# Decoding the weights of nine FFN blocks during the attention, with a stop in DRAM

## The chip, the cores and the metric

The kernel runs on one core of one Trainium2 chip. The metric is device time in microseconds (us) of one execution; before the change its median is 1493.73 us over 3 runs (1490.55 to 1495.77). A profile is one more execution, recorded by the hardware profiler.

## The reference

Three layers follow each other: causal attention in blocks of 64 (8 batches, 8 heads, 576 tokens, 64 wide), a gated convolution, and a Fourier mixing layer with an FFN.

```python
scores = where(block_i >= block_j, q @ k.T / sqrt(64), -1e9)
attn = exp(scores - max) / (sum + 1e-9)
x = attn @ v                                  # 8 x 576 x 512
gate = sigmoid(causal 5-tap convolution of x with conv_w)
x = (gate * (x @ w_val)) @ w_out
u = x + real(fft2(x))                         # over tokens and channels
un = (u - mean(u)) / sqrt(var(u) + 1e-6)
out = u + relu(un @ w_ch1) @ w_ch2            # 512 -> 2048 -> 512
```

The weights arrive as float64, so the program reads each as a pair of 32-bit words. The FFN's weights are w_ch1 (512 x 2048) and w_ch2 (2048 x 512); the hidden width of 2048 is cut into 16 blocks of 128.

## The kernel before, in words

The program has two phases. **Phase 1** is attention, gated convolution and Fourier mixing. Two heads form a pair; 32 pairs of 9 units each give 288 units (`NU`), and the loop over n at L936 walks them. One pass of the loop emits for unit n the scores (`emit_qk`, TensorE), and for units some passes behind the maximum (`emit_max`, VectorE), the exponential (`emit_exp`, ScalarE) and the transposes (`emit_t`, TensorE, copied out by ScalarE). In the ninth unit of a pair `emit_av` multiplies with the values. Before it, `emit_recip` makes the reciprocals on VectorE, and `emit_factors` transposes them on TensorE, copies them to a tile rt, and sends them through DRAM to XF. When the 4 pairs of a batch (36 units) are done, `dense(b)` is queued: the value and output products, the transforms and the store of u to DRAM (`u_d`). Its pieces are taken into the loop by `step`, so one batch's attention runs beside the previous batch's dense part. `tick` lets chains of small stages (`Chain`) go one stage further; it is called twice per unit, and so a unit has two halves. The queries of a pair are split into high and low parts in one buffer, QHL, and copied from there by DMA: to QQ by `spread` in units 4 and 8 of the pair before, to QD (two buffers, used by the ninth unit) by the last stage of `split` (L351). Kernel-wide, SyncE issues nearly all DMAs, one after the other, and each one waits in that queue for what it needs.

**Phase 2** is the FFN over 9 groups of 512 tokens. `load_u` loads u, `norm` normalises it, and the loop at L1133 goes over 16 blocks f: twelve matmuls into psh (L1143 to L1145, three for each quarter of the channels, because high and low parts are multiplied separately), relu into hh (ScalarE, L1148) and the rest hl (VectorE, L1149), and twelve matmuls into the output (L1161 to L1163) one block later. The weights stay in SBUF for all groups. They are prepared in the first group by `load_w(f)`, called two blocks ahead: a DMA brings 128 x 1024 words (rw, three buffers), `decode` turns them into 128 x 512 float32 (st, three buffers), a ScalarE copy makes the high part and a VectorE subtraction (L1055) the low one. Each block has two such tiles, W1 and W2.

`decode` puts the float32 bits together from the two words of a float64: VectorE shifts the high word (L72), adds bits of the low word (L74) and the sign and exponent bit (L76), and clears values that are too small (L84), by a magnitude that ScalarE makes of the high word (L80). That is four VectorE operations and one on ScalarE for a tile of 128 x 512.

The order of instructions on each engine is made at compile time by a planner that works by priorities (program order) and planned times. So phase 2's first loads and decodes stand between the last operations of phase 1, where memory is free for them. On the chip each engine then takes its instructions strictly in that order.

Of the kernel before, what the change touches and what calls it, by code (L numbers as in the profile page):

```python
# [8 lines left out]
F32 = mybir.dt.float32  # L9
# [8 lines left out]
def kernel(  # L18
# [46 lines left out]
    def decode(raw, dst, mag):  # L65
# [5 lines left out]
        def bits():  # L71
            nc.vector.tensor_scalar(out=d, in0=hi, scalar1=3, scalar2=0x3FFFFFFF,  # L72
                                    op0=ALU.logical_shift_left, op1=ALU.bitwise_and)
            nc.vector.scalar_tensor_tensor(out=d, in0=lo, scalar=29, in1=d,  # L74
                                           op0=ALU.logical_shift_right, op1=ALU.bitwise_or)
            nc.vector.scalar_tensor_tensor(out=d, in0=hi, scalar=-0x40000000, in1=d,  # L76
                                           op0=ALU.bitwise_and, op1=ALU.bitwise_or)

        def size():
            nc.scalar.activation(out=mag, in_=hf, func=AF.Abs)  # L80

        def guard():

            nc.vector.scalar_tensor_tensor(out=dst, in0=mag, scalar=2.0 ** -15, in1=dst,  # L84
                                           op0=ALU.is_ge, op1=ALU.mult)
        def whole():
            bits()
            guard()
        return [size, whole]
# [4 lines left out]
    f_d = [dram.tile([10, P], F32, name=f"f_d{i}") for i in range(2)]  # L94

# [6 lines left out]
    def phase1():  # L102
        with ExitStack() as c1:
# [15 lines left out]
            QD = [pa.tile([P, 2, P], F32R, name=f"QD{i}") for i in range(2)]  # L119
# [9 lines left out]
            cw = pa.tile([P, 4, 5], F32, name="cw")  # L129

# [204 lines left out]
            def split(p):  # L335
# [15 lines left out]
                def q_last():  # L351
                    for r in rs:
                        nc.sync.dma_start(out=QD[p % 2][r, :, r].bitcast(F32), in_=QHL[r, :, D:S].bitcast(F32))

# [37 lines left out]
            def emit_qk(n):  # L392
# [21 lines left out]
                for k0, w in ((0, 320), (320, 256)):  # L414
                    t = sc_tile(n)
                    mm3(t[:, 0:w], QD[p % 2][:, 0], QD[p % 2][:, 1], KP[p][:, k0:k0 + w], KL[p][:, k0:k0 + w], True, True)
# [38 lines left out]
            def emit_recip(p):  # L455

                su = sums[p]
                re = sm.tile([P, 10], F32, tag="re", name="re")
# [9 lines left out]
            def emit_factors(p):  # L468
# [7 lines left out]
                rt = sm.tile([P, P], F32, tag="rt", name="rt", bufs=2)  # L476
# [794 lines left out]
```

## Time and profile before

| | us |
|---|---|
| median of 3 runs | 1493.73 |
| lowest, highest | 1490.55, 1495.77 |
| profiled execution | 1492.41 |
| its span on the core | 1490.6 |
| TensorE busy | 1423.2 (95%) |
| VectorE busy | 829.4 (56%) |
| ScalarE busy | 645.6 (43%) |
| GpSimd busy | 310.0 (21%) |

Times inside the profile count from the start of the span. TensorE's matmuls are pipelined, so one matmul's duration is longer than the time after which the next one starts, and a busy TensorE is not one at its peak; the number of matmuls of one shape in a stretch tells more. The names of tiles are those of the program; L452 is line 452. Phase 1 ends and phase 2 begins between about 600 and 690 us; the two overlap there.

### The profile page before, as it was taken

What the parts mean: (1) busy time and instruction counts of PE and PEld (TensorE: products, weight loads), DVE (VectorE), ACT (ScalarE), POOL (GpSimd) and SP (SyncE); (2) the same over time, 40 slices, a digit from 0 to 9 for tenths busy, and PEclk for the clock granted to TensorE, in tenths of its full rate; (3) what the DMA queues carried; (4) which work ended last, traced back from release to release, by engine and by line L of the source; (5) the groups of instructions that cost most, each with busy time, mean ns of one, the idle gap of its engine ahead of it and who ended that gap; (6) DMA issues with size and microseconds to landing.
All of it is one profiled execution on the core that took longest, in us unless ns stands there. A gap on an engine that the chain in (4) does not pass through costs nothing.

```text
span 1490.6 us, 22931 instructions
## 1 busy us (share of the span) xinstructions
PE 1423.2 (95%) x8543; PEld 1205.1 (81%) x8543; DVE 829.4 (56%) x1668; ACT 645.6 (43%) x1647; POOL 310.0 (21%) x254
## 2 busy tenths in 40 slices
PE   5798999999999999987989999999999999999998
PEld 4567888989898989976768888888888888888887
DVE  6877797979797979599993322232223222222212
ACT  5678777777777777543441212121121212112110
POOL 3423132323232323221001111120111111111100
PEclk9899999999999999999999999999999999999999
DMA  7567665656565655225421010100101000010000
GB/s 216 155 165 191 158 175 151 168 152 168 153 168 152 164 156 137 87 89 173 156 84 57 0 57 0 56 2 1 57 0 57 1 29 29 0 57 0 29 0 29
DMA packets 121290, 137.22 MB, mean 92 GB/s; under 512 B 23502, under 2 KB 91356, under 8 KB 121180
## 3 DMA queue, kind: packets, MB, share of 16 engines
q1 hardware_dynamic: 120640, 135.63, 32.2%
q8 instruction: 67, 1.10, 0.3%
q14 instruction: 43, 0.35, 0.1%
q10 hardware_dynamic: 540, 0.14, 0.0%
HBM read 70.57 MB, written 19.01 MB: 60 GB/s over the span
## 4 chain that ended last, share of the span: by engine, by line
PE 69%; DVE 15%; DMA 5%; ACT 3%; POOL 3%; issue 3%; SPq 2%; DVEq 0%; ACTq 0%; POOLq 0%
PE o L1163 8%; PE o L1161 8%; PE o L1162 8%; PE psh L1144 8%; PE psh L1145 8%; PE psh L1143 8%; PE av L594 4%; PE pt L566 3%; DVE gate L621 2%; PE sc L406 2%; POOL XA L827 1%; PE sc L407 1%; PE psx L165 1%; DVE st L74 1%; DVE mx L438 1%
## 5 line engine op out<-in xcount | busy, mean ns | idle before, releaser
L1149 DVE SCALAR_TENSOR_TENSOR hl<-psh,hh 128x512 fp32r<-128x512 f32 x144 | 99.4, 690 | 392.9 <-ACT hh L1148 392.8
L1148 ACT ACTIVATE hh<-psh 128x512 fp32r<-128x512 f32 x144 | 85.9, 597 | 504.8 <-PE psh L1145 502.8
L1163 PE MATMUL o<-hl,W2H 128*128 128x512 f32 x576 | 221.0, 394 | 14.2 <-DVE hl L1149 14.0
L1145 PE MATMUL psh<-UTH,W1L 128*128 128x512 f32 x576 | 225.4, 391 | 0.9 <-DVE W1L L1055 0.9
L1143 PE MATMUL psh<-UTH,W1H 128*128 128x512 f32 x576 | 224.8, 391 | 0.8 <-ACT UTH L1108 0.8
L1144 PE MATMUL psh<-UTL,W1H 128*128 128x512 f32 x576 | 225.0, 391 | 0.4 <-DVE UTL L1109 0.4
L1161 PE MATMUL o<-hh,W2H 128*128 128x512 f32 x576 | 224.2, 389 | 0.0
L1162 PE MATMUL o<-hh,W2L 128*128 128x512 f32 x576 | 224.0, 389 | 0.0
L452 ACT ACTIVATE PB<-sc,mx 128x128 f32<-128x128 f32 (+4 forms) x320 | 166.7, 526 | 47.2 <-DVE mx L438 27.3
L566 PE MATMUL pt<-ident,PB 128*128 128x128 f32 x800 | 139.7, 282 | 10.9 <-ACT PTb L572 5.2
L1163 PEld LDWEIGHTS o<-hl,W2H 128*128 128x128 f32 x576 | 107.6, 189 | 42.4 <-DVE hl L1149 20.7
L1145 PEld LDWEIGHTS psh<-UTH,W1L 128*128 128x128 f32 x576 | 108.6, 189 | 24.1 <-DVE W1L L1055 1.3
L1143 PEld LDWEIGHTS psh<-UTH,W1H 128*128 128x128 f32 x576 | 108.6, 189 | 24.0 <-ACT UTH L1108 1.1
L1144 PEld LDWEIGHTS psh<-UTL,W1H 128*128 128x128 f32 x576 | 108.6, 189 | 23.6 <-DVE UTL L1109 0.9
L1161 PEld LDWEIGHTS o<-hh,W2H 128*128 128x128 f32 x576 | 108.1, 188 | 22.9 <-ACT hh L1148 0.5
L1162 PEld LDWEIGHTS o<-hh,W2L 128*128 128x128 f32 x576 | 108.2, 188 | 22.6
L621 DVE SCALAR_TENSOR_TENSOR gate<-XF,cw,gate 128x575 f32<-128x575 f32 (+3 forms) x128 | 121.1, 946 | 5.0 <-ACT gate L63 4.2
L566 PEld LDWEIGHTS pt<-ident,PB 128*128 128x128 f32 x800 | 100.8, 144 | 26.9 <-ACT PTb L572 12.0
L1172 POOL TENSOR_TENSOR U<-o,U 128x512 f32<-128x512 f32 x32 | 40.3, 1289 | 365.4 <-DVE o L1170 365.4
L438 DVE TENSOR_REDUCE mx<-sc 128x1 f32<-128x384 f32 (+2 forms) x192 | 104.6, 562 | 4.1 <-PE sc L167 2.1
L406 PE MATMUL sc<-K,QQ 128*128 128x256 f32 (+2 forms) x256 | 87.4, 351 | 16.3 <-DMA QQ<-QHL 13.2
L617 POOL TENSOR_TENSOR XL<-XF,XH 128x576 fp32r<-128x576 f32 x32 | 46.0, 1439 | 256.8 <-ACT XH L57 256.8
(208 smaller groups left out, 2885.8 us busy)
## 6 DMA issues: line engine op xcount, KB each, us to landing
K<-KP SPq DMA_DIRECT2D x128, 144.0 KB, 2.5
QQ<-QHL SPq DMA_DIRECT2D x128, 128.0 KB, 2.5
rw<-in_w_ch SPq DMA_DIRECT2D x32, 512.0 KB, 4.3
VV<-in_v SPq DMA_DIRECT2D x32, 320.0 KB, 3.9
qraw<-in_q SPq DMA_DIRECT2D x32, 288.0 KB, 3.3
kraw<-in_k SPq DMA_DIRECT2D x32, 288.0 KB, 3.4
out<-U SPq DMA_DIRECT2D x36, 256.0 KB, 2.0
QQ<-QHL SPq DMA_DIRECT2D x128, 64.0 KB, 2.8
```

Source lines behind the costliest of these rows:

```text
L406: nc.tensor.matmul(t[:, o:o + w], q[:, 0, m], KK[p][h][:, 0:w], start=True, stop=False)
L438: nc.vector.reduce_max(out=mx[:, j:j + 1], in_=t, axis=AX.X, negate=one)
L452: nc.scalar.activation(out=PB[i][:, k0:k0 + w], in_=t, func=AF.Exp, bias=nm, accum_out=su[:, at + j:at + j + 1])
L566: nc.tensor.transpose(ps[:, j, :], PB[i][:, (j0 + j) * P:(j0 + j + 1) * P], ident)
L621: nc.vector.scalar_tensor_tensor(out=gate[c][:, s:S], in0=XF[:, 0:S - s], scalar=cw[:, c, 4 - s:5 - s], in1=gate[c][:, s:S], op0=ALU.mult, ...
L1143: nc.tensor.matmul(ps, W1H[f][:, c, :], UTH[g][:, c, :], start=(c == 0), stop=False)
L1144: nc.tensor.matmul(ps, W1H[f][:, c, :], UTL[g][:, c, :], start=False, stop=False)
L1145: nc.tensor.matmul(ps, W1L[f][:, c, :], UTH[g][:, c, :], start=False, stop=(c == 3))
L1149: nc.vector.scalar_tensor_tensor(out=l, in0=ps, scalar=0.0, in1=h.bitcast(F32), op0=ALU.max, op1=ALU.subtract)
L1161: nc.tensor.matmul(po[t], W2H[e][:, c], h, start=(e == 0), stop=False)
L1162: nc.tensor.matmul(po[t], W2L[e][:, c], h, start=False, stop=False)
L1163: nc.tensor.matmul(po[t], W2H[e][:, c], l, start=False, stop=(e == NF - 1))
```

## The change

The two tiles of each of the blocks 0 to 8 (`KD = 9`) are decoded in phase 1, as two halves each, which makes 36 half tiles of 128 x 256. A generator, `decode_ahead`, is called twice per unit from unit 62 on (`NW`). For one half tile it issues the DMA of the words into raw_w, passes four calls, then issues the five operations of `decode` one per call, passes one more, issues a DMA of the result to a float32 tile in DRAM (`w_d`), and passes two more. There is one raw_w and one st_w. The magnitude is written over the low words. In phase 2 `load_w` loads st from `w_d` for these blocks and only splits it into high and low part; blocks 9 to 15 are decoded as before. Besides, QD has one buffer, filled in `spread` at unit 8 ahead of the QQ copies; the reciprocals' copy rt lies in XF; and the small tiles su and re have two buffers each where they had six.

```diff
-    def decode(raw, dst, mag):
+    def decode(raw, dst, mag=None):
...
+        m = lo.bitcast(F32) if mag is None else mag
+
         def size():
-            nc.scalar.activation(out=mag, in_=hf, func=AF.Abs)
+            nc.scalar.activation(out=m, in_=hf, func=AF.Abs)
...
-        return [size, whole]
+        return [shifted, low, size, high, guard] if mag is None else [size, whole]
...
+    KD = 9
+    w_d = [[dram.tile([P, D], F32, name=f"w_d{f}{z}") for z in range(2)] for f in range(KD)]
...
-            QD = [pa.tile([P, 2, P], F32R, name=f"QD{i}") for i in range(2)]
+            QD = pa.tile([P, 2, P], F32R, name="QD")
...
+            raw_w = pa.tile([P, D], I32, name="raw_w")
+            st_w = pa.tile([P, D // 2], F32, name="st_w")
...
-                return Chain(k_hi, both(k_dup, k_lo), wait, q_hi, q_lo, q_last)
+                return Chain(k_hi, both(k_dup, k_lo), wait, q_hi, q_lo)
             def spread(p, g):
...
+                if g:
+                    for r in rs:
+                        nc.sync.dma_start(out=QD[r, :, r].bitcast(F32), in_=QHL[r, :, D:S].bitcast(F32))
...
-                    sums[p] = sm.tile([P, 12], F32, tag="su", name="su")
+                    sums[p] = sm.tile([P, 12], F32, tag="su", name="su", bufs=2)
...
-                rt = sm.tile([P, P], F32, tag="rt", name="rt", bufs=2)
                 to, fd = XFS[p % NXF], f_d[p % 2]
+
+                rt = to[:, 0:P]
...
+            def decode_ahead():
+
+                for f in range(KD):
+                    for z in range(2):
+                        for c in range(2):
+                            src = ffn_words(f, z)
+                            if z:
+                                nc.sync.dma_start(out=raw_w, in_=src[:, D * c:D * c + D])
+                            else:
+                                nc.sync.dma_start(out=raw_w.rearrange("p (c f) -> p c f", c=2),
+                                                  in_=src[:, 2 * c:2 * c + 2, :])
+                            for _ in range(4):
+                                yield
+                            for stage in decode(raw_w, st_w):
+                                stage()
+                                yield
+                            yield
+                            nc.sync.dma_start(out=w_d[f][z][:, 256 * c:256 * c + 256], in_=st_w)
+                            yield
+                            yield
...
+            NW = 62
...
+                if n >= NW:
+                    next(ahead_w, None)
...
+                if n >= NW:
+                    next(ahead_w, None)
...
+            for _ in ahead_w:
+                pass
...
                     st = s3.tile([P, D], F32, tag="st", name="st")
...
+                    if f < KD:
+                        nc.sync.dma_start(out=st, in_=w_d[f][z])
+                    else:
+                        rw = rp.tile([P, 2 * D], I32, tag="r", name="rw")
+                        nc.sync.dma_start(out=rw if z else rw.rearrange("p (c f) -> p c f", c=4), in_=ffn_words(f, z))
+                        for stage in decode(rw, st, s4.tile([P, D], F32, tag="mg", name="mg")):
+                            stage()
                     nc.scalar.copy(out=h, in_=st)
```

## Rows read from the trace of the kernel before

**Rows 1.** The profile page: its first line.

```profile
span 1490.6 us, 22931 instructions
```

**Rows 2.** Table of stretches. Columns: stretch, length, each engine busy (instructions), TensorE's clock, DMA.

```profile
350.00:375.00 25.00, 24.55 (x209) 22.86 (x208) 23.51 (x58) 19.56 (x59) 6.37 (x5) 1.00 0.58 148
375.00:400.00 25.00, 25.00 (x229) 22.77 (x229) 15.82 (x39) 20.21 (x63) 4.99 (x5) 1.00 0.62 164
400.00:425.00 25.00, 24.33 (x214) 21.92 (x211) 21.46 (x50) 16.47 (x45) 11.29 (x8) 1.00 0.63 172
625.00:650.00 25.00, 22.59 (x164) 21.32 (x162) 24.00 (x49) 4.55 (x8) 5.90 (x4) 1.00 0.25 88
650.00:675.00 25.00, 23.61 (x155) 20.11 (x153) 24.73 (x46) 13.58 (x32) 7.21 (x5) 1.00 0.24 75
675.00:700.00 25.00, 19.01 (x67) 13.98 (x66) 24.27 (x34) 10.26 (x17) 5.63 (x4) 0.86 0.58 191
700.00:725.00 25.00, 23.08 (x99) 18.05 (x99) 25.00 (x46) 11.60 (x20) 0.00 (x0) 1.00 0.51 172
725.00:750.00 25.00, 22.02 (x95) 17.16 (x94) 24.36 (x45) 10.80 (x19) 0.00 (x0) 1.00 0.45 145
750.00:775.00 25.00, 20.92 (x89) 15.99 (x88) 25.00 (x45) 12.86 (x22) 0.00 (x0) 1.00 0.32 104
800.00:825.00 25.00, 25.00 (x112) 20.69 (x111) 7.46 (x12) 6.03 (x11) 1.33 (x2) 1.00 0.00 1
```

**Rows 3.** The chain of waits, 665 to 775 us: shares by line.

```profile
by line: DVE st L74 14.8%; DVE st L76 14.2%; DVE st L84 10.5%; DVE st L72 8.5%; DVE W1L L1055 7.7%; DVE W2L L1055 6.8%; DVE hl L1149 6.1%; issue 6.0%; DMA rw<-in_w_ch 3.9%; DVE UTL L1109 3.2%; DVE r L1119 3.0%; POOL XA L827 2.7%; DVE q L111
```

**Rows 4.** VectorE in order of time, one FFN block: start, length, line, operation.

```profile
698.76 0.68 DVE L1149 SCALAR_TENSOR_TENSOR hl<-psh,hh 128x512 fp32r<-128x512 f32 x1
...
700.61 0.76 DVE L72 TENSOR_SCALAR st<-rw 128x512 int32<-128x512 int32 x2
701.28 1.28 DVE L74 SCALAR_TENSOR_TENSOR st<-rw,st 128x512 int32<-128x512 int32 x2
702.48 1.29 DVE L76 SCALAR_TENSOR_TENSOR st<-rw,st 128x512 int32<-128x512 int32 x2
703.69 1.29 DVE L84 SCALAR_TENSOR_TENSOR st<-mg,st 128x512 f32<-128x512 f32 x2
704.89 0.69 DVE L1149 SCALAR_TENSOR_TENSOR hl<-psh,hh 128x512 fp32r<-128x512 f32 x1
```

**Rows 5.** Groups of instructions, 675 to 775 us: count, busy, mean ns, idle before.

```profile
L84 DVE SCALAR_TENSOR_TENSOR st<-mg,st 128x512 f32<-128x512 f32 x28 | 19.3, 712 | 0.0
L1163 PE MATMUL o<-hl,W2H 128*128 128x512 f32 x56 | 18.7, 437 | 14.1 <-DVE hl L1149 14.0
L80 ACT ACTIVATE mg<-rw 128x512 f32<-128x512 f32 x26 | 17.4, 671 | 6.3 <-DMA rw<-in_w_ch 6.3
```

**Rows 6.** DMA issues of the page: count, size, us from issue to landing.

```profile
qraw<-in_q SPq DMA_DIRECT2D x32, 288.0 KB, 3.3
```

**Rows 7.** VectorE in order of time, 646 us: two operations of 289 columns.

```profile
646.07 0.45 DVE L673 TENSOR_TENSOR GF<-gv 128x289 f32<-128x289 f32 x1
646.44 0.45 DVE L675 TENSOR_TENSOR GF<-gv 128x289 f32<-128x289 f32 x1
```

**Rows 8.** GpSimd in order of time, 573 to 576 us.

```profile
573.72 1.43 POOL L359 TENSOR_TENSOR KL<-kraw,KP 128x576 fp32r<-128x576 f32 x1 [0.96 <-ACT KP L57]
```

**Rows 9.** VectorE in order of time: two taps of the convolution.

```profile
574.46 1.31 DVE L621 SCALAR_TENSOR_TENSOR gate<-XF,cw,gate 128x574 f32<-128x574 f32 x1
...
579.71 0.72 DVE L621 SCALAR_TENSOR_TENSOR gate<-XF,cw,gate 128x572 f32<-128x572 f32 x1
```

**Rows 10.** Groups of VectorE's instructions, 200 to 575 us.

```profile
L673 DVE TENSOR_TENSOR GF<-gv 128x289 f32<-128x289 f32 x20 | 9.2, 458 | 0.0
```

**Rows 11.** Waits, 200 to 575 us: who for whom, us in total, times, longest.

```profile
PEld rt L475 <- DVE re L465: 5.2, 11, 0.6
```

**Rows 12.** SyncE's queue in order of time, at 281 us.

```profile
281.36 1.24 SPq L353 DMA_DIRECT2D QD<-QHL  x2
```

More of the change, by code (lines that the diff above doesn't have):

```diff
@@ L94, with ffn_words @@
     f_d = [dram.tile([10, P], F32, name=f"f_d{i}") for i in range(2)]
+    KD = 9
+    w_d = [[dram.tile([P, D], F32, name=f"w_d{f}{z}") for z in range(2)] for f in range(KD)]
+    def ffn_words(f, z):
+        if z:
+            return w_ch2[f * P:(f + 1) * P, :].bitcast(I32)
+        return w_ch1[:, f * P:(f + 1) * P].bitcast(I32).rearrange("(c p) f -> p c f", p=P)
     cst = ctx.enter_context(tc.tile_pool(name="cst", bufs=1))
@@ L457, in emit_recip @@
                 su = sums[p]
-                re = sm.tile([P, 10], F32, tag="re", name="re")
+                re = sm.tile([P, 10], F32, tag="re", name="re", bufs=2)
                 nc.vector.tensor_tensor(out=su[:, 4:6], in0=su[:, 10:11].to_broadcast([P, 2]),
@@ L490, in emit_recip_near @@
                 su = sums[p]
-                re = sm.tile([P, 10], F32, tag="re", name="re")
+                re = sm.tile([P, 10], F32, tag="re", name="re", bufs=2)
                 both = su[:, 0:12].rearrange("p (h c) -> p h c", h=2)[:, :, 2 * g:2 * g + 2]
@@ L906, in phase1 @@
             nc.gpsimd.memset(PB[8][:, S:640], 0.0)
-            for t in QD + [QQ[h][g][rs[1 - h], 1, :] for h in range(2) for g in range(2)]:
+            for t in [QD] + [QQ[h][g][rs[1 - h], 1, :] for h in range(2) for g in range(2)]:
                 nc.gpsimd.memset(t.bitcast(F32), 0.0)
@@ L915, in phase1 @@
             next(prep)
+            ahead_w = decode_ahead()
             credit = 0.0
@@ L1042, in load_w @@
             def load_w(f):
-                for src, h, l in (
-                    (w_ch1[:, f * P:(f + 1) * P].bitcast(I32).rearrange("(c p) f -> p c f", p=P), W1H[f], W1L[f]),
-                    (w_ch2[f * P:(f + 1) * P, :].bitcast(I32), W2H[f], W2L[f]),
-                ):
-                    rw = rp.tile([P, 2 * D], I32, tag="r", name="rw")
-                    nc.sync.dma_start(out=rw if h is W2H[f] else rw.rearrange("p (c f) -> p c f", c=4), in_=src)
-                    if h is W1H[f]:
+                for z, (h, l) in enumerate(((W1H[f], W1L[f]), (W2H[f], W2L[f]))):
+                    if z == 0:
                         h, l = h.rearrange("p c f -> p (c f)"), l.rearrange("p c f -> p (c f)")
                     st = s3.tile([P, D], F32, tag="st", name="st")
-                    for stage in decode(rw, st, s4.tile([P, D], F32, tag="mg", name="mg")):
-                        stage()
+                    if f < KD:
[5 more added lines that the diff above has]
+                            stage()
                     nc.scalar.copy(out=h, in_=st)
```

16 lines of the change are left out of this document (8 added, 8 removed).

## The prediction

> **What bounds the kernel now.** The span first: 1490.6 us [rows 1], inside a profiled execution of 1492.4 us, 1.3 us under the median of the three runs (1493.73). The sum below is made against 1492.4 and moved by those 1.3 us at its end. I read the table of stretches next, because the two halves of the kernel have different limits.
>
> In the attention, from 200 to 575 us, one batch (36 units of work) takes 75 us and the pattern of three stretches repeats (five times; one stands in the rows): TensorE is busy 24.55, 25.00 and 24.33 of 25 us, while VectorE is busy 23.51, 15.82 and 21.46 us, ScalarE 19.56, 20.21 and 16.47, GpSimd 6.37, 4.99 and 11.29 [rows 2]. So TensorE sets the pace, VectorE is at 60.8/75 = 81%, and in one third of each batch already at 94%.
>
> At the border to the FFN this turns round. From 625 to 775 us VectorE is busy 24 to 25 of every 25 us, and from 675 us TensorE runs 67, 99, 95 and 89 matmuls in stretches in which it later runs 112 [rows 2]. In the steady FFN one matmul costs 25/112 = 0.223 us, so the missing 45, 13, 17 and 23 are 10.0 + 2.9 + 3.8 + 5.1 = 21.8 us of TensorE time. (Clock: the granted share is 0.86 in the first of these stretches, between its two levels, and 1.00 in the others; the cost of that is inside the 10.0.) From 625 to 675 us it is idle 2.4 + 1.4 = 3.8 us more. The chain of waits names the cause: of 665 to 775 us the decode lines L74, L76, L84 and L72 hold 48%, and W1L, W2L and hl on the same engine 21% [rows 3]. One FFN block shows it: from one hl to the next 6.13 us pass without a gap on VectorE (698.76 to 704.89), of which 4.28 us (700.61 to 704.89) are the decode of two tiles [rows 4]. TensorE needs 24 x 0.223 = 5.36 us for a block, and it waits for hl 14.0 us in 100 us [rows 5].
>
> **What the change takes from the FFN.** Nine blocks lose their decode: 9 x 4.28 = 38.5 us of VectorE, and 18 of 32 absolute values on ScalarE (0.67 each [rows 5]). What stays for such a block is 1.85 us of VectorE. Between 675 and 775 us VectorE is busy 98.6 us [rows 2]; there the decode of about 13 tiles falls away (28 touch that stretch, one of them begun before it [rows 5]; 14 are left), 13 x 2.14 = 27.8, leaving 70.8 us beside 100 - 21.8 = 78.2 us of TensorE work. TensorE becomes the bound, if the seven blocks that still decode are started early. I expect that: their weight tiles have places of their own, and VectorE has 5.36 - 1.85 = 3.5 us free in each of blocks 0 to 8, 9 x 3.5 = 31 us, against 7 x 4.28 = 30 us of decode. This just fits, so I leave 4 us in waits. At the border, 5 tiles x 2.14 = 10.7 us of VectorE disappear before 675; TensorE can gain no more than 3.8 us there and I take 2. **Gain: 21.8 - 4 + 2 = 20 us**; bounds 25.6 (everything) and 13 (only what is lost up to 725 us, if the late blocks still run at VectorE's pace). The new loads are covered: 256 KB land within the 3.3 us of a 288 KB load [rows 6]; with copy and subtract (0.6 each, a third of 1.85) a buffer is held 4.5 us, three buffers give a tile every 1.5 us, and a block needs one every 2.7. Without that cover each tile would cost up to 3.3 us.
>
> **What it adds to the attention.** 36 half tiles, each 12 half-units of the loop long, that is six units: 432 of the 466 calls between unit 62 and the end, so nothing is left over after it. Six fall on a batch, two on a third. Each has four VectorE operations and one on ScalarE. No row shows them at 256 columns. Below, half of 4.28/2: 1.07 us. Nearer is a two-operand operation on 289 columns, after which the next one starts 0.37 us later [rows 7]; three of these and half of L72 (0.67/2/2 = 0.17 [rows 4]) make 1.28. Above, GpSimd: at 573.72 it starts an operation of 1.43 us [rows 8]; a tap on VectorE at 574.46 takes 1.31 where another of nearly the same width takes 0.72 [rows 9], as if it began when GpSimd ended at 575.15. GpSimd is busy 22.65/75 = 30% [rows 2], half its operation is 0.72 us, so each of the four operations may wait 0.30 x 0.72 = 0.21 us on average, and a half tile costs up to 1.28 + 0.86 = 2.14 us. The Trainium skill ("SBUF — State Buffer", section "SBUF: two separate sides") speaks against the change here: a port pair shared by VectorE and GpSimd is locked for a whole instruction, and the other engine fully blocks. The rows at 573.72 and 574.46 agree with it, and by that rule the 2.14 would be the price and not the 1.28.
>
> I take 1.3 us, the nearer rows, because the 289-column operation itself keeps its short time in the attention: 458 ns on average over 20, against 0.45 alone [rows 10]. A third then gets 2.6 us: 26.1, 18.4 and 24.1 us of VectorE. Two thirds stay under 25 and the fullest goes 1.1 over. There TensorE waits: already now its weight load for rt stands 11 times on VectorE's reciprocals, 5.2 us in all [rows 11], and an in-order queue that is fuller lengthens such waits. I put 1.5 us on each batch; six batches are decoded in: **9 us**. Bounds: 0 (the backlog is carried into the next third; the batch sums to 68.6 of 75) and 42 (below). ScalarE gets 6 x 0.34 = 2 us per batch at 75% load: in the 1.5.
>
> The small edits I cost at nothing, each with its cover. The QD copies move from the query's split to unit 8, ahead of four QQ copies in SyncE's queue, and wait for that unit's score matmuls; they take 1.24 us to issue [rows 12]. With at most one unit (75/36 = 2.1 us) of waiting, 4 x 0.62 us for QQ's own issue and 3.3 us to land, QQ arrives after 9.2 us; it is needed five units (10.4 us) later. If that cover is gone, each late us is paid by 31 pairs. Two DMAs per half tile are about 1 us of SyncE in six units (12.5 us). The store waits for VectorE's last step, issued a unit before; behind it stand the K copies and QQ. The load is placed two units (4.2 us) ahead of its use and lands in 3.3; a late one stops all that is behind it on VectorE. The reciprocals' row in XF waits for taps six units old; the fewer su and re buffers wait for readers of a pair ago.
>
> **The rivals.** *A, fully absorbed:* no wait in the attention, the gain 20 to 25: 1467 to 1474. For it: 68.6 of 75. Against: the third at 26.1. *B, slower: VectorE takes over the attention.* Each half tile costs 2.14, a third gets 4.3 us, nothing is carried from one third into the next because every queue is in order, and VectorE fills no more than the 94% it reaches today: (23.5 + 4.3)/0.94 = 29.6 and (21.5 + 4.3)/0.94 = 27.4, that is 4.6 + 2.4 = 7.0 us per batch, 42 us in six, minus 20: 1516. It decides from 20/6 = 3.3 us per batch; between there and 7.0 lies 1494 to 1516, its middle 1505. For it: the 94%, the port. Against: VectorE has 9 us free in the light third. *C, half the gain:* blocks 9 to 15 still at 6.13 us, the gain 13 or less, the cost 9: 1490. For it: 30 us of decode in 31 free. The case that nothing of the change takes effect I exclude: the loop has the calls to run it.
>
> **How the numbers follow.** 1492.4 - 20 + 9 = 1481.4; against the median 1482.7: I predict 1483. Chances: this forecast 0.50 (1475 to 1489), A 0.12, C 0.20 (mostly within 0.3%), B 0.18. A measurement of this kernel can tell about 0.3%, 4.5 us: faster means under 1489.2, slower over 1498.2. Faster: 0.50 + 0.12 + 0.03 = 0.65; the same: 0.15 of C and 0.02 of B = 0.17; slower: 0.02 + 0.16 = 0.18. The range, 1470 to 1504, leaves out the better half of A and the upper half of B.
>
> **What would show it.** In the FFN's first group, matmuls per 25 us should be near 112 from some 675 us on, and the wait for hl (14.0 us) nearly gone; if it comes back after the ninth block, C is right. In the attention a batch should take 76.5 us instead of 75; at 75 A is right, over 78 B. The four new operations should sum to 1.3 us a half tile; over 2 tells of GpSimd. The prediction is wrong if TensorE begins to wait for K or QQ copies behind the new stores, or VectorE for the raw words.

## The result, and the profile after

The changed kernel takes 1502.39 us (median of 6 runs, 1500.59 to 1503.52) where the kernel before took 1495.15 (6 runs on the same chip, 1490.55 to 1497.53). The ratio is 1.0051, with a 95% interval of 1.0035 to 1.0067. The time lies inside the predicted range, near its upper end, and above the old one: slower by half a per cent where faster was forecast.

The first line of the page after, beside [rows 1]:

```profile
span 1501.5 us, 23301 instructions
```

The spans of the two profiled executions differ by 10.9 us, the medians by 7.2: executions of one kernel lie some us apart, and what is read below from one execution of each kernel is good to that. One event splits the span: the last score matmul of the attention (operands KP and QD), on TensorE in order of time, before and then after. Columns: start, length, engine, line, operation.

```profile
608.37 0.28 PE L167 MATMUL sc<-KP,QD 128*128 128x256 f32 x1
```

```profile
641.43 0.28 PE L186 MATMUL sc<-KP,QD 128*128 128x256 f32 x1
```

With its length the attention's scores end at 608.6 us before and at 641.7 after: **33.1 us lost**. From there to the end of the span 882.0 us pass before and 859.8 after: **22.2 us won**. The same two numbers, called the scores' end and the rest below, are used for every experiment.

**Where the gain is.** Table of stretches after, columns as in [rows 2]:

```profile
675.00:700.00 25.00, 22.34 (x148) 19.52 (x146) 22.16 (x41) 17.24 (x39) 4.08 (x4) 1.00 0.41 120
700.00:725.00 25.00, 24.12 (x120) 19.54 (x119) 24.73 (x37) 8.20 (x14) 5.75 (x4) 1.00 0.49 153
725.00:750.00 25.00, 25.00 (x112) 20.72 (x111) 25.00 (x46) 12.32 (x22) 0.00 (x0) 1.00 0.49 156
750.00:775.00 25.00, 25.00 (x112) 20.70 (x111) 23.09 (x40) 12.73 (x22) 0.00 (x0) 1.00 0.17 55
775.00:800.00 25.00, 25.00 (x111) 20.67 (x111) 9.14 (x10) 3.68 (x6) 5.04 (x4) 1.00 0.09 31
```

From 725 us on TensorE runs 112 matmuls per 25 us, its steady pace, at a granted clock of 1.00, although VectorE is still full up to 775. Before it ran 95 and 89 there. The wait for hl, 14.0 us within 100 us in [rows 5], is 0.9 us over the whole kernel (group of the page; the last number is what ended the idle time):

```profile
L1212 PE MATMUL o<-hl,W2H 128*128 128x512 f32 x576 | 224.5, 390 | 1.1 <-DVE hl L1198 0.9
```

And the chain of waits from 695 to 800 us, in which decode lines held 48% in [rows 3], is now for 83% TensorE's six groups of matmuls:

```profile
by line: PE psh L1193 14.3%; PE psh L1192 14.2%; PE o L1212 13.9%; PE psh L1194 13.8%; PE o L1210 13.6%; PE o L1211 13.6%; issue 2.7%; DVE XA L846 2.0%; DVE r L1168 1.5%; PE pss L184 1.5%; DVE W1L L1104 1.4%; PE pss L186 1.3%; PE pss L185 1
```

**Where the loss is.** One batch of the attention now takes 80 us (79.4 to 82.6 over five of them, by the same score matmul 36 units apart) instead of 75 (74.5 to 77.1). One such batch by stretches, beside the three attention lines of [rows 2]:

```profile
424.00:449.00 25.00, 23.03 (x194) 20.76 (x193) 24.92 (x51) 16.57 (x46) 11.78 (x7) 1.00 0.62 172
449.00:474.00 25.00, 22.52 (x190) 20.52 (x189) 24.13 (x62) 18.52 (x57) 4.98 (x4) 1.00 0.64 176
474.00:504.00 30.00, 29.26 (x263) 26.25 (x262) 22.50 (x58) 22.90 (x69) 6.43 (x5) 1.00 0.68 188
```

VectorE fills its stretches (24.92 and 24.13 of 25 us) and TensorE has gaps (23.03 and 22.52) where before it was busy for 24.3 to 25.0. VectorE's busy time per batch goes from 60.8 to 71.55 us, and TensorE's idle time from 1.1 us in 75 to 5.2 in 80.

The new operations themselves, groups of VectorE's instructions from 200 to 600 us (count, busy, mean ns, idle before). L72, L76, L80 and L91 are the four of a half tile:

```profile
L91 DVE SCALAR_TENSOR_TENSOR st_w<-raw_w,st_w 128x256 f32<-128x256 f32 x30 | 23.4, 779 | 1.0 <-ACT raw_w L87 0.7
L76 DVE SCALAR_TENSOR_TENSOR st_w<-raw_w,st_w 128x256 int32<-128x256 int32 x30 | 16.4, 548 | 0.2
L80 DVE SCALAR_TENSOR_TENSOR st_w<-raw_w,st_w 128x256 int32<-128x256 int32 x30 | 15.1, 504 | 0.1
L72 DVE TENSOR_SCALAR st_w<-raw_w 128x256 int32<-128x256 int32 x30 | 12.6, 419 | 5.8 <-DMA raw_w<-in_w_ch 5.5
```

Their means sum to 2.25 us a half tile. A mean that is so far above the length of most instances hides two lengths. VectorE and GpSimd in order of time, around one of them:

```profile
445.95 0.41 DVE L80 SCALAR_TENSOR_TENSOR st_w<-raw_w,st_w 128x256 int32<-128x256 int32 x1
446.29 0.14 DVE L458 TENSOR_REDUCE mx<-mx 128x1 f32<-128x2 f32 x1
446.35 0.44 DVE L678 SCALAR_TENSOR_TENSOR gv<-gate,psv 128x288 f32<-128x288 f32 x1
446.71 0.81 DVE L640 SCALAR_TENSOR_TENSOR gate<-XF,cw,gate 128x575 f32<-128x575 f32 x1
447.44 0.14 DVE L691 COPY gv<-gv 128x1 f32<-128x1 f32 x1
447.50 1.58 DVE L91 SCALAR_TENSOR_TENSOR st_w<-raw_w,st_w 128x256 f32<-128x256 f32 x1
449.01 0.45 DVE L692 TENSOR_TENSOR GF<-gv 128x289 f32<-128x289 f32 x1
```

```profile
446.75 2.05 POOL L374 TENSOR_TENSOR KL<-kraw,KP 128x576 fp32r<-128x576 f32 x1 [2.34 <-ACT KP L57]
```

L80 takes 0.41 us with GpSimd idle, and the next operation starts 0.34 us after it. L91, of the same size, starts at 447.50 while GpSimd's subtraction runs until 448.80, and ends at 449.08, 0.28 us after it. So do all ten L91 that start under a GpSimd operation between 200 and 620 us. (0.28 is less than the 0.42 that L91 takes undisturbed; where in the operation the wait lies isn't shown.) GpSimd's own operation starts 0.04 us after a tap and takes 2.05 us, where one took 1.43 in [rows 8]. In the trace before, from 200 to 600 us, the nine of these subtractions that start under a tap take 1.79 to 2.00 us and the twelve others 1.42 to 1.43.

### The profile page after: what moved, and what is told of

It reads as the page before. It is cut to its first block, busy times and chain, and to the rows that moved or that the text cites. A ratio compares the mean times of both kernels' runs of the same rounds, so it can differ in the third digit from the quotient of the medians.

```text
span 1501.5 us, 23301 instructions
## 1 busy us (share of the span) xinstructions
PE 1433.1 (95%) x8543; PEld 1209.4 (81%) x8543; DVE 855.4 (57%) x1740; ACT 645.9 (43%) x1665; POOL 311.1 (21%) x253
## 4 chain that ended last, share of the span: by engine, by line
PE 65%; DVE 14%; issue 6%; DMA 6%; ACT 5%; POOL 2%; SPq 2%; DVEq 0%; ACTq 0%; POOLq 0%
PE o L1212 8%; PE psh L1193 8%; PE o L1210 8%; PE psh L1192 8%; PE o L1211 8%; PE psh L1194 8%; DVE gate L640 3%; PE av L613 3%; PE pt L585 3%; PE sc L424 2%; ACT PB L470 2%; PE sc L425 1%; DVE mx L456 1%; DMA QQ<-QHL 1%; PE psx L184 1%
## 5 line engine op out<-in xcount | busy, mean ns | idle before, releaser
L1212 PE MATMUL o<-hl,W2H 128*128 128x512 f32 x576 | 224.5, 390 | 1.1 <-DVE hl L1198 0.9
L470 ACT ACTIVATE PB<-sc,mx 128x128 f32<-128x128 f32 (+4 forms) x320 | 166.6, 526 | 51.7 <-DVE mx L456 27.2
L585 PE MATMUL pt<-ident,PB 128*128 128x128 f32 x800 | 143.7, 281 | 11.7 <-ACT PTb L591 5.6
L640 DVE SCALAR_TENSOR_TENSOR gate<-XF,cw,gate 128x575 f32<-128x575 f32 (+3 forms) x128 | 126.1, 985 | 3.8 <-ACT gate L63 3.6
L424 PE MATMUL sc<-K,QQ 128*128 128x256 f32 (+2 forms) x256 | 91.3, 367 | 16.9 <-DMA QQ<-QHL 11.0
```

The lines of the kernel that those rows point to most:

```text
L424: nc.tensor.matmul(t[:, o:o + w], q[:, 0, m], KK[p][h][:, 0:w], start=True, stop=False)
L470: nc.scalar.activation(out=PB[i][:, k0:k0 + w], in_=t, func=AF.Exp, bias=nm, accum_out=su[:, at + j:at + j + 1])
L585: nc.tensor.transpose(ps[:, j, :], PB[i][:, (j0 + j) * P:(j0 + j + 1) * P], ident)
L640: nc.vector.scalar_tensor_tensor(out=gate[c][:, s:S], in0=XF[:, 0:S - s], scalar=cw[:, c, 4 - s:5 - s], in1=gate[c][:, s:S], op0=ALU.mult, ...
L1212: nc.tensor.matmul(po[t], W2H[e][:, c], l, start=False, stop=(e == NF - 1))
```

## The experiments

Two theories stood against each other for the 33 us, with two side issues:

- **Port**: the operations wait for GpSimd, as in the rows just shown, so that a half tile costs about 2 us of a VectorE that has little left, and the batch grows.
- **Everything but the port**: the edits that make room, the DMAs in SyncE's queue, the operations' plain length, or ScalarE's share of the work.
- Whether words, stores or ScalarE's magnitude come late, and so hold up everything behind them on VectorE.
- Whether it matters in which part of a batch a half tile stands.

All runs in one table; each ratio is to runs of the kernel before taken beside it. The batches are the five of 36 units each from pair 8 on; "rest" is the span less the scores' end.

| kernel | median us | ratio to before, 95% | scores' end | batches | rest |
|---|---|---|---|---|---|
| before | 1495.15 | | 608.6 | 77.1 75.3 74.7 74.6 74.5 | 882.0 |
| after | 1502.39 | 1.0051 [1.0035, 1.0067] | 641.7 | 82.6 80.5 79.4 80.0 79.9 | 859.8 |
| e1_room | 1496.62 | 1.0018 [1.0006, 1.0029] | 610.9 | about 75 | 882.1 |
| e2_dma | 1480.44 | 0.9912 [0.9881, 0.9943] | 616.9 | 79.2 75.6 74.6 75.4 76.0 | 861.1 |
| e3_reduce | 1481.49 | 0.9916 [0.9894, 0.9939] | 623.2 | 79.7 78.3 76.4 75.9 77.3 | 858.9 |
| e4_light4 | 1493.29 | 0.9992 [0.9981, 1.0003] | 628.1 | 77.6 81.3 79.9 77.8 75.8 | 865.3 |
| e8_nosize | 1505.9 | 1.0078 [1.0055, 1.0101] | 644.5 | 82.5 80.0 80.4 80.3 81.3 | 861.4 |
| e6_early | 1498.86 | 1.0034 [1.0023, 1.0046] | 635.0 | 81.7 79.3 78.6 77.2 77.8 | 860.7 |
| e9_light4b | 1493.41 | 0.9996 [0.9983, 1.0008] | 625.6 | 77.8 77.9 76.6 79.5 78.2 | 864.6 |
| e10_tail2 | 1489.70 | 0.9969 [0.9956, 0.9983] | 608.9 | about 75 | 878.2 |
| e12_quiet_after | 1470.04 | 0.9842 [0.9825, 0.9858] | 608.8 | 76.9 77.2 76.9 75.4 75.7 | 860.9 |
| e13_quiet_before | 1480.97 | 0.9926 [0.9908, 0.9944] | 594.8 | 76.2 73.8 73.5 73.5 73.5 | 882.9 |
| e5_even4 | 1491.22 | 0.9979 [0.9963, 0.9995] | 625.8 | 82.6 80.2 76.9 74.8 74.9 | 864.6 |
| e11_tail3 | 1487.46 | 0.9958 [0.9944, 0.9973] | 607.5 | about 74.5 | 875.7 |

### The parts of the change, one after the other: e1_room, e2_dma, e3_reduce

Three versions of the changed kernel, each with one part more. e1_room keeps only the edits that make room (QD, rt, su and re, the two tiles):

```diff
-    KD = 9
+    KD = 0
```

> The changed kernel with no block decoded ahead: only the edits that make room stay (one QD buffer filled at unit 8, rt inside XF, two su and re buffers). Theory V (VectorE's own operations in the attention are the cost): nothing is lost here, 1490 to 1498 us, a batch of 36 units takes 74.6 us as before. Theory Q (SyncE's queue and the single buffers are the cost, because QD now stands ahead of the QQ copies and waits for the ninth unit's scores): a batch takes 77 to 80 us, the kernel 1510 to 1530 us.

e2_dma has the loads, the stores and the FFN's side, without the five operations; st_w is filled once with a constant:

```diff
                             for stage in decode(raw_w, st_w):
-                                stage()
                                 yield
...
+            nc.vector.memset(st_w, 0.03)
```

> The changed kernel in which the five decode operations of the attention are left out: the 36 loads of words and the 36 stores stay, and the FFN loads what was stored, a constant (so its output is not the reference's). Theory V: a batch takes 75 us again and the FFN keeps its gain of about 23 us, 1469 to 1476 us. Theory Q (SyncE's issues and the DMA traffic): a batch stays at 78 to 80 us, 1490 to 1502 us.

e3_reduce puts four reductions over the 256 words in the place of the four operations; ScalarE's operation stays:

```diff
-                            for stage in decode(raw_w, st_w):
-                                stage()
+                            def look(j, raw=raw_w[:, 1::2].bitcast(F32)):
+                                nc.vector.reduce_max(out=st_w[:, j:j + 1], in_=raw, axis=AX.X)
+                            for j, stage in enumerate(decode(raw_w, st_w)):
+                                if j == 2:
+                                    stage()
+                                else:
+                                    look(j)
                                 yield
...
+            nc.vector.memset(st_w, 0.03)
```

> The changed kernel in which each of the four VectorE operations of a half tile is replaced by a maximum over the same 256 high words (one SBUF input; its result goes to one column of st_w), so the FFN's weights of nine blocks are not the reference's; loads, stores and ScalarE's operation stay. The reductions are as long as the decode operations are when GpSimd is idle (0.41 us), and of the 24 reductions of a unit pair in the attention none is lengthened by GpSimd. Theory V-time (the time of four more operations in VectorE's queue is the cost): a batch takes 79 to 80 us, 1495 to 1503 us. Theory V-port (waiting for GpSimd, of these operations and of those behind them, is most of the cost): a batch takes 76 to 77 us, 1478 to 1486 us, with 1.3 us of VectorE per half tile instead of 2.0.

e1_room came out where Theory V had it and e3_reduce where V-port had it; e2_dma, at 1480.44 us, lies between its two ranges. The last scores of e1_room, e2_dma and e3_reduce:

```profile
610.59 0.28 PE L186 MATMUL sc<-KP,QD 128*128 128x256 f32 x1
```

```profile
616.64 0.28 PE L186 MATMUL sc<-KP,QD 128*128 128x256 f32 x1
```

```profile
622.95 0.28 PE L186 MATMUL sc<-KP,QD 128*128 128x256 f32 x1
```

By the scores' end the parts are: room 610.9 - 608.6 = **2.3 us**, DMAs 616.9 - 610.9 = **6.0**, four operations of the same count that don't meet GpSimd, with ScalarE's, 623.2 - 616.9 = **6.3**, and what the real operations add to these 641.7 - 623.2 = **18.5**. Together 33.1. The medians show the last step as clearly: e3_reduce 1481.49, after 1502.39, 21 us apart; between e2_dma and e3_reduce they differ by 1 us only, and their spans by 4.1. Each end is read from one execution, and the four of e2_dma lie from 1477.20 to 1486.48 us, so the 2.3, the 6.0 and the 6.3 are uncertain by some us each.

The reductions are a fair stand-in by length. Group of VectorE's instructions in e3_reduce, 200 to 600 us:

```profile
L908 DVE TENSOR_REDUCE st_w<-raw_w 128x1 f32<-128x256 f32 x126 | 48.6, 402 | 10.9 <-DMA raw_w<-in_w_ch 10.6
```

Four of 402 ns are 1.6 us a half tile, about what the four real ones take undisturbed (below, 1.54). Sorted by whether a GpSimd operation was running when they started (VectorE and GpSimd in order of time, 200 to 620 us), the reductions take 394 ns with it (41 of them) and 405 without (87). One of them, and the GpSimd operation beside it:

```profile
512.88 0.40 DVE L908 TENSOR_REDUCE st_w<-raw_w 128x1 f32<-128x256 f32 x1
```

```profile
512.09 1.43 POOL L374 TENSOR_TENSOR KL<-kraw,KP 128x576 fp32r<-128x576 f32 x1 [0.28 <-ACT KP L57]
```

In the same run the taps of the convolution, L640, take 1221 with and 776 without. So the two kinds of operation stand beside the same GpSimd work, and one of them doesn't wait for it.

The same sorting of the changed kernel's four operations, 32 of each from 200 to 620 us:

| operation | GpSimd running at its start: count, mean ns | not running: count, mean ns |
|---|---|---|
| L72 | 10, 712 | 22, 287 |
| L76 | 6, 1202 | 26, 416 |
| L80 | 12, 635 | 20, 415 |
| L91 | 10, 1618 | 22, 417 |

38 of 128 meet GpSimd, 30%, and these are longer by 0.62 us on average. That is 0.30 x 0.62 x 4 = 0.74 us a half tile on top of 0.287 + 0.416 + 0.415 + 0.417 = 1.54 us.

### GpSimd made quiet: e12_quiet_after, e13_quiet_before

The port from its other side. GpSimd's two large subtractions (KL and XL, which read two tiles each) become fills that read nothing, in the changed kernel and in the kernel before:

```diff
-                    nc.gpsimd.tensor_tensor(out=kl, in0=kraw[p], in1=kh.bitcast(F32), op=ALU.subtract)
+                    nc.gpsimd.memset(kl.bitcast(F32), 0.0)
...
-                    nc.gpsimd.tensor_tensor(out=xl, in0=XF, in1=xh.bitcast(F32), op=ALU.subtract)
+                    nc.gpsimd.memset(xl.bitcast(F32), 0.0)
```

> The changed kernel in which GpSimd's two subtractions per pair (the low parts of K and of x) are replaced by GpSimd filling the same tiles with zero, an operation that reads nothing; the low parts are lost, so the output is only roughly the reference's. These two are 8 x 1.43 = 11.4 of GpSimd's 22.6 us per batch; the four butterflies per batch stay. To be compared with e13_quiet_before. Theory V-port (decode operations wait while GpSimd holds a shared port): about half of the 21 us between decode operations and reductions goes, and the difference of the two quiet kernels is 0 to -4 us, where the plain ones differ by +8. Theory V-time: the difference stays at +6 to +10 us.

> The kernel before with the same replacement of GpSimd's two subtractions per pair (the low parts are lost). TensorE has the pace there and VectorE's taps wait less for GpSimd, so both theories expect the same time or a little less: 1486 to 1494 us. It is the other half of the pair with e12_quiet_after.

With GpSimd quiet the same change is a gain: 1470.04 against 1480.97, 10.9 us faster instead of 7 slower. The sign turns. The attention loses 608.8 - 594.8 = 14.0 us instead of 33.1, and the rest gains 22.0, as it did. The effect is much larger than was expected of this pair (a difference of 0 to -4 us; and of the kernel before alone, a gain of 0 to 8, where the ratio of 0.9926 makes it 11). Less the 2.3 and the 6.0 of room and DMAs, 5.7 us of the 14.0 are left for the operations, close to the 6.3 that the reductions cost.

The last scores of e12_quiet_after and e13_quiet_before:

```profile
608.56 0.28 PE L186 MATMUL sc<-KP,QD 128*128 128x256 f32 x1
```

```profile
594.53 0.28 PE L167 MATMUL sc<-KP,QD 128*128 128x256 f32 x1
```

Groups of e12_quiet_after, 200 to 600 us: the fill, and the operation that was longest.

```profile
L374 POOL MEMSET KL<- 128x576 f32 x20 | 11.7, 587 | 152.5 <-PE sc L186 119.0 <-PE sc L185 33.4
L91 DVE SCALAR_TENSOR_TENSOR st_w<-raw_w,st_w 128x256 f32<-128x256 f32 x31 | 18.2, 588 | 0.5 <-ACT raw_w L87 0.4
```

The fill takes 587 ns where the subtraction took 1595 (L374, 20 of them, after), and L91's mean falls from 779 to 588. The fills also end sooner than the subtractions, and VectorE's other operations meet GpSimd less; what this is worth by itself stands in both kernels of the pair, and it was not taken apart from the port. Nor do the runs tell how much of the delay is VectorE's waiting and how much GpSimd's. The operations that GpSimd still has (additions for XA, splits of XOOL and XEEL) keep some of the waits: 6 of L91's 31 still met one and took 1309 ns.

### Late words, stores and magnitudes: e8_nosize, e6_early, e9_light4b

L87, ScalarE's magnitude, writes over the low words and so waits for L76; ScalarE stands still for that 12.2 us from 200 to 600 us:

```profile
L87 ACT ACTIVATE raw_w<-raw_w 128x256 f32<-128x256 f32 x30 | 13.4, 446 | 16.5 <-DVE st_w L76 12.2 <-issue 4.0
```

e8_nosize leaves this operation out, and the guard reads the high words as they are:

```diff
-        m = lo.bitcast(F32) if mag is None else mag
+        m = hf if mag is None else mag
...
-            nc.scalar.activation(out=m, in_=hf, func=AF.Abs)
+            if mag is not None:
+                nc.scalar.activation(out=m, in_=hf, func=AF.Abs)
```

> The changed kernel without ScalarE's operation in the attention: the magnitude of the high words is not taken, and the last decode step compares the high words themselves, so negative weights of nine blocks become zero and the output is not the reference's. The four VectorE operations stay as they are. In the changed kernel this ScalarE operation writes over the low words and so waits for VectorE's second step (10.5 us in 25 operations); in the run with reductions it had no such wait. Theory V-port (the port alone makes the difference between decode operations and reductions): the last scores end within 4 us of the changed kernel's 641.7, the kernel takes 1497 to 1503 us. Theory A (ScalarE held by VectorE, and the exponentials behind it, make most of that difference): the last scores end near 625 us, 1480 to 1488 us.

It isn't faster (1505.9, above both ranges; scores' end 644.5 against 641.7, within the 4 us of Theory V-port). So ScalarE's wait is real but isn't what costs the 33 us. Why the kernel gains nothing without it isn't shown.

e6_early asks for the next half tile's words as soon as the last reader of raw_w is issued, three calls sooner:

```diff
+                words(0)
+                for k, (f, z, c) in enumerate(halves):
                     for _ in range(4):
                         yield
                     for stage in decode(raw_w, st_w):
                         stage()
                         yield
+                    words(k + 1)
                     yield
```

> The changed kernel in which the next half tile's words are asked for right after the last step that reads raw_w, three half-units earlier than before. VectorE waited 5.5 us for words between 270 and 590 us; its own loads took 3.6 us to land. If these waits lie on the path they are worth 5 to 9 us: 1493 to 1498 us. If VectorE's port waits are what sets the pace, they are hidden: 1499 to 1503 us.

1498.86 against 1502.39, between the two expected ranges, and scores that end at 635.0 instead of 641.7: the wait for the words is worth some 3.5 us of the median (2.5 by the two ratios), and the kernel is still slower than before.

### The place in the batch: e4_light4, e9_light4b, e5_even4

Four blocks, 16 half tiles. e4_light4 decodes in units 30 to 35 and 0 to 8 of each batch alone, around the stretch in which VectorE was busy for only 15.82 of 25 us [rows 2]:

```diff
-    KD = 9
+    KD = 4
...
-                if n >= NW:
+                if n >= NW and (n % 36 >= 30 or n % 36 < 9):
```

> The changed kernel with four blocks decoded ahead instead of nine (16 half tiles), and only in the units of a batch in which VectorE has most room in the kernel before (30 to 35 and 0 to 8 of 36). If the cost comes from the stretches in which VectorE was already full (the place decides), the attention loses under 4 us and about 10 us of the FFN's first group are gained: 1484 to 1490 us. If each half tile costs the same wherever it stands (34 us for 36, 0.94 us each), the attention loses 15 us and the kernel takes 1495 to 1502 us.

e9_light4b is the same with the words asked for early, as in e6_early, and the magnitude two calls later:

```diff
-        return [shifted, low, size, high, guard] if mag is None else [size, whole]
+        return [shifted, low, high, lambda: None, size, lambda: None, guard] if mag is None else [size, whole]
```

> The run with four blocks in VectorE's lighter units again, but with the words asked for earlier (as in e6_early) and ScalarE's magnitude two half-units behind the step that it has to wait for. In e4_light4 VectorE waited 9.9 us for words and ScalarE 13.2 us for VectorE, and the last scores ended 19.5 us late. If those two waits are that delay, the last scores end near 614 us and the kernel takes 1477 to 1484 us. If the delay is the port and the place, it stays at 1490 to 1495 us.

e5_even4 has four blocks too, one half tile after the other from unit 62 on:

```diff
-    KD = 9
+    KD = 4
```

> The changed kernel with four blocks decoded ahead instead of nine, one after the other from unit 62 on, whatever VectorE has to do there; the pair of e4_light4, which has the same 16 half tiles in the lighter units. If the place in the batch decides, this loses more than e4_light4 and takes 1497 to 1503 us. If each half tile costs about the same wherever it stands among the units 62 to 280 (34 us in 36, so 15 in 16, beside 17 us gained by four blocks), it takes 1490 to 1496 us, the same as e4_light4.

e4_light4 lies between its two ranges, and its scores end 19.5 us late, where under 4 or 15 had been expected. e9_light4b came out where the delay is the port and the place, and e5_even4 where each half tile costs about the same. Less the 2.3 us of room, a half tile costs (628.1 - 608.6 - 2.3)/16 = 1.07 us in the light stretch, (625.8 - 608.6 - 2.3)/16 = 0.93 where the sixteen follow one another, and (33.1 - 2.3)/36 = 0.86 in the changed kernel. The light stretch isn't cheaper. In e5_even4 the two batches after the decode's end are back at 74.8 and 74.9, so but for some tenths the cost belongs to the half tiles and to nothing that lasts.

What e4_light4 and e9_light4b show at raw_w is waits of an in-order queue. Idle time of the engine before the instructions of this tile, what ended it, us and times; e4_light4 first, then e9_light4b:

```profile
  DVE st_w L76: 13.2, 8
  DMA raw_w<-in_w_ch: 9.9, 8
```

```profile
  DMA w_d<-st_w: 9.2, 6
  DVE st_w L76: 7.7, 5
```

In the first, VectorE stands eight times on the words; with the words early it stands on the store of the last half tile, which has the only st_w: 9.9 us became 9.2. Whether the light stretch would be cheaper with more buffers was not tried, and stays open.

### Where it costs nothing: e10_tail2, e11_tail3

The kernel before, with none of the edits that make room. Two blocks are decoded in the last units of the attention (277 to 294), when the buffers of raw, K0, K1, KP and KL are no longer needed, and lie there; the words of half tile k + 2 are asked for behind the last step of half tile k. The FFN's side is that of the changed kernel:

```diff
+    KD = 2
...
+                for k, (f, z, c) in enumerate(halves):
+                    st = kp.tile([P, S], F32, tag=("K0", "KP")[k % 2], name="st_w")[:, 0:256]
+                    mg = kp.tile([P, S], F32, tag=("K1", "KL")[k % 2], name="mg_w")[:, 0:256]
+                    for j, stage in enumerate(decode(raws[k], st, mg, True)):
+                        stage()
+                        if j == 3:
+                            words(k + 2)
+                        if j % PER == PER - 1:
+                            yield
...
+            NW = 277
```

> The kernel before, with two blocks decoded ahead in the last units of the attention (277 to 294) and in buffers that the last pairs have left, so that none of the edits that make room is needed; 8 half tiles, each with its own tile for the magnitude, words asked for two half tiles ahead. From 600 to 625 us VectorE is busy 12.3 of 25 us in the kernel before and GpSimd 3.7. If half tiles are cheap where VectorE and GpSimd both have room, the last scores end within 3 us of 608.6, two blocks give some 10 us of the FFN's first group, and the kernel takes 1483 to 1488 us. If each half tile costs 0.9 us wherever it stands, 1490 to 1495 us.

e11_tail3 has three blocks and passes three calls per half tile (the edit is against e10_tail2):

```diff
-    KD = 2
+    KD = 3
...
-                        if j % PER == PER - 1:
+                        if j != 1:
                             yield
```

> As e10_tail2, with three blocks instead of two in the last units of the attention, three half-units per half tile. e10_tail2 gained 4.5 us, and its loss on TensorE that is left lies between 725 and 775 us (11.4 us, the late blocks). If VectorE has room for four more half tiles at the attention's end, a third block takes 3 to 5 us more off: 1483 to 1488 us. If the room is used up, the stores and the transforms' last steps come later and it takes 1488 to 1494 us.

The scores end at 608.9 and 607.5, where they ended at 608.6 before, and the rest is shorter by 3.8 and 6.3 us. Some 10 were expected of e10_tail2's two blocks, and its 1489.70 us lie between its two ranges. e11_tail3, at 1487.46 us and a ratio of 0.9958 [0.9944, 0.9973], is faster than both kernels. It leaves most of the FFN's loss where it was. Its table of stretches, beside [rows 2]:

```profile
725.00:750.00 25.00, 23.61 (x101) 18.21 (x100) 25.00 (x45) 12.06 (x21) 0.00 (x0) 1.00 0.50 158
750.00:775.00 25.00, 21.90 (x88) 17.31 (x87) 21.80 (x38) 11.53 (x20) 1.47 (x2) 0.93 0.10 31
```

101 and 88 matmuls, with 112 to be had. In the first stretch VectorE is full, and the late blocks still go at its pace. In the second it is busy for 21.80 us and TensorE's granted clock is 0.93, between its two levels, so a part of what is missing there may be the clock. With four blocks decoded ahead the rest is shorter by 16.7 to 17.4 us (e4_light4, e5_even4, e9_light4b), with nine by 22.2.

## Why the prediction was wrong

**The FFN: right.** A gain of 20 us was forecast, 22.2 is what the rest gained, and the signs named for it came: 112 matmuls from 725 us on, a wait for hl that is nearly gone, and no return of it behind the ninth block. That refutes rival C. The 4 us that I left in waits were too many: from 725 to 800 us TensorE isn't idle, and the 3.6 us for which it still is lie between the scores' end and 725, at the border (2.66 and 0.88 of them in the first two stretches shown).

**The price of a half tile: the step that failed.** "I take 1.3 us, the nearer rows, because the 289-column operation itself keeps its short time in the attention: 458 ns on average over 20". The mean was read rightly and proves nothing: in the trace before, none of these 20 started while a GpSimd operation ran. So they were no sample of what an operation put elsewhere meets. The upper bound of 2.14 was nearly the price. Its undisturbed part, 1.28, is 1.54 by durations and about 1.26 by pitch (each starts some 0.07 us before the end of the one ahead, as at 445.95 and 446.29); its wait, 0.86, is 0.74. Together 2.0; by busy time, (71.55 - 60.8)/6 = 1.8 us. Its working was right as well: 30% of the operations meet GpSimd, as its busy share said, and wait 0.62 us, not far from half an operation, 0.72. The tap of [rows 9] that stretched beside [rows 8] was the row to go by: an operation with the same kind of operands, at a time when GpSimd ran. The trace before has more of it: of the 81 taps from 200 to 575 us, 44 start under a GpSimd operation and take 1.11 us on average, the other 37 take 0.79. The rule of the Trainium skill that the prediction weighed ("SBUF — State Buffer", section "SBUF: two separate sides") agrees with the runs: L91 at 447.50 ends 0.28 us behind GpSimd's operation, and reductions, with one tensor read, don't wait (394 and 405 ns). The same section of the Trainium skill counts an operation with a single tensor to the lock too if it runs in a mode that takes both ports; L72 (712 against 287 ns) fits that, but which mode it runs in no run here shows.

**Turning VectorE's time into the batch's: the second failure.** The step let two thirds of a batch absorb their share and put 1.5 us on the batch. With the right price the same step gives 12 us more VectorE work per batch in 14.2 us of room; two of the three thirds would overrun, by 23.5 + 4.0 - 25 = 2.5 and 21.5 + 4.0 - 25 = 0.5 us: 3 us a batch, 18 in six. Measured were 5.4 a batch (79.9 against 74.5 in the last of the five) and 33.1 in all, of which the operations have 18.5 + 6.3 = 24.8. So the step falls some 7 us short even at the right price. The waits seen on TensorE (rt for the reciprocals, psv for gv, sc for PB: 7.0, 5.2 and 2.3 us from 270 to 590) show who hands the delay on:

```profile
PE rt L493 <- DVE re L483: 7.0, 9, 1.6
PE psv L184 <- DVE gv L678: 5.2, 7, 0.8
PE sc L424 <- ACT PB L470: 2.3, 3, 0.9
```

In the trace before, TensorE's matmuls have no wait for gv from 200 to 575 us, and the one for re, from 270 to 572, is

```profile
PE rt L475 <- DVE re L465: 1.3, 4, 0.3
```

For K or QQ copies, which the prediction named, TensorE doesn't wait in these stretches. In the fullest stretch VectorE is now busy for 24.92 of 25 us, so what it owes to TensorE comes later. The three waits sum to 14.5 us over about four batches; the last four of the five lose 20.7, and the rest of that isn't accounted for.

**"The small edits I cost at nothing": 8.3 us.** Room took 2.3 and the DMAs 6.0. The covers that I named were each long enough by the rows; what they left out the runs show only in part. In e1_room TensorE's wait for re, 1.3 us before, is 3.7 from 270 to 590 us, and there the 2.3 may lie; which of the edits does it wasn't tried. VectorE does stand for the words (5.5 us before L72 after, 10.6 before the reductions of e3_reduce), which the prediction named as what would make it wrong: in the changed kernel the loads land after 3.4 us in the median and 4.7 at the longest, where the cover was 4.2. Asking earlier gives 3.5 us back. But this wait lies in the operations' 24.8 and not in the 6.0, for in e2_dma no operation reads the words, so nothing can wait for them, yet the 6.0 are there. They aren't spread evenly over the DMAs: the first of the five batches takes 79.2 us against 77.1, the next three 74.6 to 75.6 against 74.6 to 75.3, the last 76.0 against 74.5. A hint is GpSimd, whose XL subtraction stands 27.2 us until a store to w_d has ended (group of e2_dma, 200 to 600 us):

```profile
L636 POOL TENSOR_TENSOR XL<-XF,XH 128x576 fp32r<-128x576 f32 x22 | 31.5, 1431 | 162.5 <-ACT XH L57 129.4 <-DMA w_d<-st_w 27.2 <-DMA qraw<-in_q 5.3
```

XL reads no word of w_d, and such a wait is put down to what came last; whether this delay reaches TensorE was not tried. The mechanism of the 6.0, and that of the 2.3, stay open.

**Rival B was the mechanism.** VectorE takes over the attention, by the port. The sign named for it, a batch of over 78 us, came with 80. Its price was 7.0 us a batch, measured are 5.4; it put the point from which it decides at 3.3, and the middle of its band, 1505, is close to the 1502.39. It had a chance of 0.18. That the time still lies within 1470 to 1504 is owed to the width of that range, not to the mechanism that the forecast went by. Against it I set the 9 us that VectorE has free in the light third; e4_light4 and e5_even4 show that a half tile there costs no less. Rival A, full absorption, fell with that. (Two slips in the sums change nothing: A's lower end, with the 1.3 us added as elsewhere, is 1468 and not 1467, and the times for QQ add up to 9.1 us and not 9.2.)

By the terms: -20 and +9 were forecast, -22.2 and +33.1 came, of which 18.5 is the port, 6.3 the operations' plain length with their wait for the words, and 8.3 what was costed at nothing. Without the 18.5 the span would have been 1490.6 - 22.2 + 14.6 = 1483.0, a gain of 7.6 us where 11 were forecast. That e3_reduce has a span of 1482.1 is no second proof, because the 14.6 is read from it.

## What to carry to other kernels

A mean of an operation in the busy stretch is a price only if its instances meet the other engine's work as often as the new ones will; look at each start against the neighbour's instructions, and if none overlaps, take the row of one that does. VectorE, 81% busy on average, with an in-order queue full of others' inputs, had no 19% to give here: the change lengthened each batch by half of what it added to VectorE's busy time (5.4 of 10.75 us). Work that must be moved goes first to where the receiving engine's clients are ending (the last units of the attention), and if it must stand beside GpSimd, in a kind of operation whose length GpSimd doesn't change (here the reductions).

## What the runs showed of the hardware

- An operation of 417 ns on two tiles of 256 columns takes 1618 ns on average when it starts under a GpSimd operation; a reduction of 402 ns, with one tile read, isn't lengthened at all. The single-tile L72 (integer shift and mask) is: 712 against 287.
- An operation that reads one tensor from SBUF and one that a matmul left in PSUM isn't lengthened either: gv (gate and psv, 288 columns) takes 441 ns under GpSimd (16 of them) and 442 without (25), in the trace before from 200 to 575 us.
- It goes both ways: GpSimd's subtraction took 2.05 us behind a tap that began 0.04 us sooner, and 1.42 to 1.43 in the trace before where it started under no such tap.
- GpSimd is busy for only 30% of the attention, and yet the kernel before runs at 0.9926 [0.9908, 0.9944] of its time, about 11 us faster, when two of its subtractions per pair are fills that read nothing. Whether it is the reading or the shorter length that counts there was not tried.
- 72 DMAs more, with nothing computed on them, moved the scores' end by 6.0 us (one execution of each kernel), although the DMA share was no more than 0.73 in the three stretches from 350 to 425 us (0.58 to 0.63 before, [rows 2]).
